# Two gate rows formed as columns and spread over the partitions through a DRAM row, the last features of two tiles activated and turned together, and the order list made anew

## The chip, the cores and the metric

The kernel runs on one core of a Trainium2 chip. The metric is the device time of one execution in microseconds (us). Every ratio below compares runs in the fast state on the same chip.

## The reference, cut to what matters

One layer: a linear attention with a learned feature map, then a gated feed-forward network (FFN), both with a normalisation that a vector `c` modulates, and both with a gate on their way back into `x`.

```python
mod = (_silu(c) @ w_mod).reshape(c.shape[0], 6, 1, -1)   # c: 1x512, w_mod: 512x3072
sa, ca, ga, sb, cb, gb = (mod[:, 0], mod[:, 1], mod[:, 2], mod[:, 3], mod[:, 4], mod[:, 5])
h = _layernorm(x) * (1 + ca) + sa                        # x: 1x2048x512
x = x + ga * _A_ref(h, ...)                              # attention, 32 heads of 16, ends in @ wo
h = _layernorm(x) * (1 + cb) + sb
x = x + gb * (_silu(h @ w_gate) * (h @ w_up)) @ w_down   # 1376 features inside
```

The two gates `ga` and `gb` are rows of 512 numbers, the same for all 2048 tokens. The 1376 inner features of the FFN are ten blocks of 128 and a last block of 96, "the last features".

## The kernel before

Tokens go through in 16 tiles of 128. In the first phase GpSimd makes the key features `phik` of every tile, TensorE accumulates key by value (`kv_ps`) and forms the query projections (`q_front`). Then come the attention of a tile (`attend`, into the output bank `four_ps` of TensorE), its projection by `wo`, and the FFN. Every step is declared as an operation with the engine that takes it. A long list, `ORDER`, fixes for each engine the order of its operations, and a helper fills planned gaps of TensorE with multiplications of ones.

A gate is needed on all partitions. The kernel before gets it there in the matmul itself, whose stationary operand is one column repeated 128 times, so that every output partition holds the same row:

```python
gab = const.tile([P, 2, D], BF16, name="gab")

def gate(gi):
    col0 = (2 * D, 5 * D)[gi]
    t = bank("fold")
    def f():
        for k in range(KD):                                   # KD = 4, D = 512
            nc.tensor.matmul(t()[:], lhsT=silucT[:, k:k + 1].to_broadcast([P, P]),
                             rhs=wmod_sb[:, k, col0:col0 + D], start=(k == 0), stop=(k == KD - 1))
    pl.op("PE", ..., fn=f)
    pl.op("ACT", ..., fn=lambda: nc.scalar.copy(gab[:, gi, :], t()[:]))
...
for k in range(KD):                    # the first gate is multiplied into wo, on GpSimd or VectorE
    eng.tensor_tensor(wo_sb[:, k, :], wo_sb[:, k, :], gab[:, 0, :], op=ALU.mult)
```

The last features of a tile come out with tokens on partitions and have to be turned, that is transposed, which a DMA transfer does:

```python
def ffn_tail(unit, guT):               # unit: one tile or two
    for q in range(w):                 # each tile by itself
        ps_ = bank("gu", (P, 2 * lastf))
        ...                            # 8 matmuls of 96 columns: gate and up
        ... nc.scalar.activation(sg()[:], ps_()[:, 0:lastf], ACT.Silu)
        ... nc.vector.tensor_tensor(gul()[:, 0:lastf], ps_()[:, lastf:2 * lastf], sg()[:], op=ALU.mult)
        ... nc.sync.dma_start(gu()[:, q * P:(q + 1) * P], gul()[:], transpose=True)
```

All loads, stores and turns here but three small ones (64, 16 and 1 KB, on ScalarE's queue) go through SyncE's DMA queue, one issued behind the other. The weights `wo`, `wg`, `wu` and `wd` are loaded from about 36 us on.

The softmax here doesn't subtract the row's maximum and nothing guards it: scores larger than these inputs give would overflow.

## Time and profile before

| what | value |
|---|---|
| time, median of three runs | 208.27 us |
| span of the profiled run (it took 209.14 us, 0.9 us over the median) | 207.3 us |
| GpSimd: first to last key feature | 19.93 to 56.20, 36.27 us |
| first scaling of `wo` on GpSimd | 56.20 us |
| first FFN matmul (L948) | 71.79 us |
| from there to the end | 207.3 - 71.79 = 135.5 us |

Since the start of an execution varies, points of time in two traces can differ by a microsecond for no reason; stretches are compared where it matters.

First, SyncE's timeline, with the start, the duration of the issue and the transfer, where the big weight loads are issued:

```profile
36.70 0.50 SPq L317 DMA_DIRECT2D wg_sb<-in_B_w_gate_dram  x1
37.24 0.51 SPq L317 DMA_DIRECT2D wu_sb<-in_B_w_up_dram  x1
37.79 7.96 SPq L317 DMA_DIRECT2D wd_sb<-in_B_w_down_dram  x2
```

Second, the DMA view, its total for the window from 42 to 54 us, in which these loads run:

```profile
DMA packets 2087, 3.20 MB, mean 266 GB/s; under 512 B 64, under 2 KB 1440, under 8 KB 2086
```

SyncE is held for 8 us by the issue of `wd`, where `wg` and `wu` took 0.5 us each; the data flow at 266 GB/s, which includes a slack end after all has landed.

### The profile page before, as it was taken

How to read it: one execution, taken by the hardware profiler on the slowest of the kernel's cores; microseconds unless marked ns; L12 is line 12 of the kernel's file. 1: busy time of each engine (PE TensorE's matmuls, PEld its weight loads, DVE VectorE, ACT ScalarE, POOL GpSimd, SP SyncE). 2: the span in 40 equal slices, each digit the busy share in tenths (PEclk: the TensorE clock that was granted, in tenths of full speed). 3: DMA queues.
4: the chain of work that ended last, by engine and by line, in shares of the span. 5: the costliest groups of instructions: out<-in, count | busy, mean ns of one | idle time of the engine just before them, and what ended most of it. 6: DMA issues, size and time to landing. Idle time of an engine off the chain costs nothing.

```text
span 207.3 us, 4949 instructions
## 1 busy us (share of the span) xinstructions
PE 202.4 (98%) x1876; PEld 140.0 (68%) x1876; DVE 143.1 (69%) x351; ACT 114.0 (55%) x244; POOL 131.0 (63%) x172
## 2 busy tenths in 40 slices
PE   7999999999999999999999999999999999999994
PEld 2764656454555698785887876879675787698752
DVE  6699899999676886999789687887467222322232
ACT  2689999998789974335452542422532564044300
POOL 1069999899991546689678793677749254061451
PEclk9999999999999999999999999999999999999999
DMA  5996993797000011231611233202321330020012
GB/s 176 335 389 119 321 191 87 275 406 254 4 0 0 3 25 36 51 81 26 91 32 28 58 83 81 57 0 60 79 62 28 79 85 3 13 66 27 0 34 68
DMA packets 34025, 19.76 MB, mean 95 GB/s; under 512 B 25073, under 2 KB 30674, under 8 KB 34002
## 3 DMA queue, kind: packets, MB, share of 16 engines
q1 hardware_dynamic: 33712, 19.38, 33.5%
q8 instruction: 14, 0.23, 0.5%
q10 hardware_dynamic: 290, 0.08, 0.2%
q14 instruction: 9, 0.07, 0.1%
HBM read 11.58 MB, written 2.10 MB: 66 GB/s over the span
## 4 chain that ended last, share of the span: by engine, by line
PE 92%; DMA 2%; ACT 1%; POOL 1%; DVE 1%; SPq 0%; issue 0%; DVEq 0%
PE one_ps L906 34%; PE one_ps L978 18%; PE one_ps L852 7%; PE one_ps L613 6%; PE one_ps L673 6%; PE one_ps L617 5%; PE four_ps L781 4%; PE one_ps L948 3%; PE kv_ps L1046 2%; DMA wqkv_sb<-in_A_wqkv_dram 2%; PE kv_ps L649 2%; PE one_ps L447 1%; PE one_ps L551 1%; PE one_ps L540 1%; ACT e L624 1%; POOL phik L642 1%
## 5 line engine op out<-in xcount | busy, mean ns | idle before, releaser
L978 PE MATMUL one_ps<-wd_sb,gu 128*128 128x512 bf16 (+2 forms) x176 | 41.0, 372 | 0.0
L906 PE MATMUL one_ps<-hT,wg_sb 128*128 128x256 bf16 (+1 forms) x400 | 41.0, 251 | 0.0
L906 PE MATMUL one_ps<-hT,wu_sb 128*128 128x256 bf16 (+1 forms) x400 | 40.9, 251 | 0.0
L913 ACT ACTIVATE sg<-one_ps 128x512 bf16<-128x512 f32 (+1 forms) x42 | 23.7, 576 | 27.6 <-PE one_ps L906 26.4
L906 PEld LDWEIGHTS <-wg_sb 128*128 128x128 bf16 x400 | 32.7, 98 | 4.8
L906 PEld LDWEIGHTS <-wu_sb 128*128 128x128 bf16 x400 | 32.9, 98 | 4.2
L916 DVE TENSOR_TENSOR gu<-one_ps,sg 128x512 bf16<-128x512 f32 (+1 forms) x26 | 16.6, 640 | 22.1 <-PE one_ps L906 12.8
L642 POOL TENSOR_TENSOR phik<-e,R 128x1024 bf16<-128x1024 bf16 x16 | 30.5, 1930 | 1.1 <-ACT eT L679 0.7
L922 POOL TENSOR_TENSOR gu<-usb,sg 128x512 bf16<-128x512 bf16 x16 | 18.5, 1155 | 16.8 <-ACT sg L913 13.3
L978 PEld LDWEIGHTS <-gu 128*128 128x128 bf16 (+1 forms) x187 | 17.7, 98 | 15.0
L384 DVE BATCH_NORM_STATS2 st<-x_c 128x6 f32<-128x512 bf16 x32 | 21.3, 682 | 1.4 <-DMA x_c<-in_A_x_dram 1.1
L994 POOL TENSOR_TENSOR ot<-x_c,fg 128x512 bf16<-128x512 bf16 (+1 forms) x14 | 15.7, 1118 | 8.8 <-DVE fg L990 8.8
L839 POOL TENSOR_TENSOR o<-o 128x512 bf16<-128x512 bf16 x14 | 16.1, 1154 | 7.6 <-DVE o L819 7.1
L819 DVE TENSOR_TENSOR o<-four_ps,A 128x512 bf16<-128x512 f32 x32 | 20.5, 683 | 0.0
L634 DVE TENSOR_REDUCE S<-e 128x64 f32<-128x1024 bf16 x16 | 19.0, 1194 | 0.6 <-ACT e L624 0.4
L624 ACT ACTIVATE e<-one_ps 128x512 bf16<-128x512 f32 x32 | 17.7, 631 | 1.6 <-POOL phik L642 1.0
L990 DVE TENSOR_TENSOR fg<-one_ps,gab 128x512 bf16<-128x512 f32 (+1 forms) x16 | 10.7, 672 | 11.5 <-PE one_ps L978 10.8
L679 ACT ACTIVATE eT<-one_ps 128x512 bf16<-128x512 f32 x32 | 17.5, 628 | 1.4 <-PE one_ps L673 1.3
L920 ACT CAST usb<-one_ps 128x512 bf16<-128x512 f32 x16 | 9.3, 586 | 16.3 <-PE one_ps L906 14.4
L852 PE MATMUL one_ps<-wo_sb,oT 128*128 128x512 bf16 x64 | 16.1, 379 | 0.0
L617 PE MATMUL one_ps<-wqkv_sb,hT 128*128 128x512 bf16 x64 | 15.9, 379 | 0.1
L673 PE MATMUL one_ps<-hT,Wq 128*128 128x512 bf16 x64 | 15.6, 379 | 0.1
(117 smaller groups left out, 311.2 us busy)
## 6 DMA issues: line engine op xcount, KB each, us to landing
wmod_sb<-in_w_mod_dram SPq DMA_DIRECT2D x2, 1024.0 KB, 7.0
out_dram<-ot SPq DMA_DIRECT2D x15, 128.0 KB, 2.0
wg_sb<-in_B_w_gate_dram SPq DMA_DIRECT2D x1, 1376.0 KB, 8.3
wu_sb<-in_B_w_up_dram SPq DMA_DIRECT2D x1, 1376.0 KB, 11.3
wd_sb<-in_B_w_down_dram SPq DMA_DIRECT2D x1, 1280.0 KB, 14.4
x_c<-in_A_x_dram SPq DMA_DIRECT2D x4, 256.0 KB, 4.7
wmod_sb<-in_w_mod_dram SPq DMA_DIRECT2D x4, 256.0 KB, 5.7
wqkv_sb<-in_A_wqkv_dram SPq DMA_DIRECT2D x2, 512.0 KB, 7.1
```

Of the source, the lines that this page charges most:

```text
L384: pl.op("DVE", r=reads, w=[st6], us=0.6, fn=lambda: nc.vector.bn_stats(st6()[:], src))
L617: nc.tensor.matmul(v()[:], lhsT=hT[c_i][k][:, cols], rhs=wqkv_sb[:, k, 2 * D:3 * D], start=(k == 0), stop=(k == KD - 1))
L624: nc.scalar.activation(e()[:, :, sg].rearrange("p g h f -> p g (h f)"), pk()[:].rearrange("p (g n) -> p g n", g=G), ACT.Exp, scale=(1.0, - ...
L634: pl.op("DVE", r=[e], w=[Ss], us=1.14, fn=lambda: nc.vector.tensor_reduce(Ss()[:], e()[:].rearrange("p g s h f -> p (g s h) f"), axis=AX.X ...
L642: pl.op("POOL", r=[e, R], w=[bphik[i]], us=1.92, fn=lambda: nc.gpsimd.tensor_tensor(bphik[i]()[:].rearrange("p g s h f -> p (g s h) f"), e ...
L673: nc.tensor.matmul(pq()[:], lhsT=Wq2[:, k, j * P:(j + 1) * P], rhs=hT[c_i][k][:], start=(k == 0), stop=(k == KD - 1))
L819: nc.vector.tensor_tensor(o2()[:, sg].rearrange("p j (h d) -> p j h d", d=DH), ndv()[:, :, sg, 0:P].rearrange("p j (h d) -> p j h d", d=DH ...
L852: nc.tensor.matmul(a()[:], lhsT=oT()[:, j, :], rhs=wo_sb[:, j, :], start=(j == 0), stop=(j == KD - 1))
L906: nc.tensor.matmul(ps_()[0:fsz, q * n:(q + 1) * n], lhsT=wt[:, k, m * P:m * P + fsz], rhs=h2[k], start=(k == 0), stop=(k == KD - 1))
L913: pl.op("ACT", r=[g, btab], w=[sg], us=0.08 + 0.41 * L / CW, fn=lambda: nc.scalar.activation(sg()[0:fsz, 0:L], g()[0:fsz, 0:L], ACT.Silu))
L922: pl.op("POOL", r=[usb, sg], w=[gu], us=0.17 + 0.98 * L / CW, fn=lambda: nc.gpsimd.tensor_tensor(gu()[0:fsz, 0:L], usb()[0:fsz, 0:L], sg() ...
L978: nc.tensor.matmul(fp()[:], lhsT=b()[0:fsz, c0:c0 + P], rhs=wd_[0:fsz, m, wcs], start=(m == 0), stop=(m == FM - 1))
```

## The change

The intent is to take matmul time from TensorE and small steps from the other engines. A gate becomes 16 one-column matmuls, which give it as four columns of 128 (`gcol`, 128x4). A store writes these as a row of 512 numbers into DRAM, and a load reads that row back onto all 128 partitions. In units of two tiles the last features share one activation, one multiplication and one turn. The order list was made anew.

```diff
+    grow = dram.tile([2, D], BF16, name="grow")              # a row in DRAM for each gate
     def gate(gi):
-        t = bank("fold")
+        t = bank("fold", [P, KD])
+        col = const.tile([P, KD], BF16, name=f"gcol{gi}")
             for k in range(KD):
-                nc.tensor.matmul(t()[:], lhsT=silucT[:, k:k + 1].to_broadcast([P, P]), rhs=wmod_sb[:, k, col0:col0 + D], ...)
+                for j in range(KD):
+                    nc.tensor.matmul(t()[:, j:j + 1], lhsT=wmod_sb[:, k, col0 + j * P:col0 + (j + 1) * P],
+                                     rhs=silucT[:, k:k + 1], ...)
-        pl.op("ACT", ..., fn=lambda: nc.scalar.copy(gab[:, gi, :], t()[:]))
+        pl.op([("ACT", ...), ("DVE", 0.12, lambda: nc.vector.tensor_copy(col[:], t()[:]))], ...)
+        nc.sync.dma_start(grow[gi:gi + 1, :].rearrange("a (j p) -> p (a j)", p=P), col[:])
+        nc.sync.dma_start(gab[:, gi, :], grow[gi:gi + 1, :].broadcast_to([P, D]))
     def ffn_tail(unit, guT):
-        for q in range(w):                                   # 16 activations, multiplications and turns
+        ps_ = bank("gu", (P, w * 2, lastf))                  # 10 of each
         ...
+        nc.scalar.activation(sg()[:, 0:w, :], ps_()[:, 0:2 * w:2, :], ACT.Silu)
+        nc.vector.tensor_tensor(gul()[:, 0:w, 0:lastf], ps_()[:, 1:2 * w:2, :], sg()[:, 0:w, :], op=ALU.mult)
+        nc.sync.dma_start(gu()[:, 0:w * P]..., gul()[:, 0:w, :]..., transpose=True)
     ... (buffer counts; the order list replaced whole)
```

In the store, partition p holds the elements p, 128 + p, 256 + p and 384 + p of the row. So no two neighbours in DRAM come from the same partition: the 1 KB goes out as 512 separate writes of two bytes.

## The prediction

> **What bounds the kernel now.** I read the page first: engine shares, the slices, the chain that ended last. Then the chain in order of time, the lines of the operations that the change touches, and GpSimd's and SyncE's timelines.
>
> ```profile
> span 207.3 us, 4949 instructions
> PE 202.4 (98%) x1876; PEld 140.0 (68%) x1876; DVE 143.1 (69%) x351; ACT 114.0 (55%) x244; POOL 131.0 (63%) x172
> ...
> PE 92%; DMA 2%; ACT 1%; POOL 1%; DVE 1%; SPq 0%; issue 0%; DVEq 0%
> ```
>
> TensorE is busy from end to end, and 92% of the chain is TensorE's own work. No other engine is above 69%. So a change pays if it takes matmul time away, or time in which TensorE fills a wait. The kernel does fill: its helper at L1046 multiplies ones into an unused bank wherever its plan sees a gap, so a busy TensorE can hide a wait. The chain in order of time shows the gates (L692) and the two fills that matter here:
>
> ```profile
> 33.09 0.78 PE one_ps L492 x32
> ...
> 53.10 0.86 PE one_ps L692 x4
> ...
> 56.21 0.52 PE kv_ps L649 x16
> 56.73 0.86 PE one_ps L692 x4
> ...
> 70.36 0.65 PE one_ps L1046 x3
> 71.01 0.23 PE one_ps L447 x4
> 71.23 0.50 PE four_ps L781 x8
> 71.73 0.22 PE one_ps L1046
> ```
>
> Each gate is four 512-column matmuls, 0.86 us, and both lie on the chain. L492 forms the other modulation values as columns already: 32 one-column matmuls in 0.78 us. After the first projections TensorE fills for 0.65 + 0.22 = 0.87 us; from 72 us to 203 us no fill remains, the stretch is matmuls back to back.
>
> The first phase has a second bound. GpSimd's timeline:
>
> ```profile
> 19.93 1.93 POOL L642 TENSOR_TENSOR phik<-e,R 128x1024 bf16<-128x1024 bf16 x1
> 21.84 2.28 POOL L434 TENSOR_SCALAR xn<-x_c,ln_mv,ln_nmr 128x512 bf16<-128x512 bf16 x3
> ...
> 46.77 9.48 POOL L642 TENSOR_TENSOR phik<-e,R 128x1024 bf16<-128x1024 bf16 x5 [0.30 <-PE kv_ps L649]
> 56.20 4.49 POOL L736 TENSOR_TENSOR wo_sb<-wo_sb,gab 128x512 bf16<-128x512 bf16 x4
> ```
>
> From 19.93 to 56.20 it makes the 16 key features with hardly a gap, and the last one frees the last key-value accumulation (56.21 on the chain). TensorE and GpSimd end this phase together. The third bound, the end, is the last matmul near 204 us, two VectorE steps and a store.
>
> The operations of the last features (L952, L954, L957):
>
> ```profile
> L952 ACT ACTIVATE sgl<-one_ps 128x96 bf16<-128x96 f32 x16 | 4.0, 249 | 15.6 <-PE one_ps L948 15.5
> L954 DVE TENSOR_TENSOR gul<-one_ps,sgl 128x96 bf16<-128x96 f32 x16 | 3.9, 243 | 7.1 <-ACT sgl L952 7.0
> L957 SPq DMA_TRANSPOSE gu<-gul x16: 1093/1182/1235, 79.8 to 185.2; - x16
> ```
>
> They are on three engines with room, and none of the three shows on the chain; TensorE never waits there for a turned tile.
>
> **What the Trainium skill says.** (1) "TensorE: Matmul & The Clock Gate", section "Wait — 56ns, not 53.3ns?": a warm matmul starts N / 2.4 GHz plus about 2.5 ns after the one before, and never less than about 25 ns. The trace agrees: 0.86 / 4 = 215 ns at 512 columns, 0.78 / 32 = 24 ns at one. (2) "DMA: Bandwidth & Descriptors", section "Anatomy of one DMA — SWDGE (gpsimd) path": a transfer has a fixed cost of about 2 us, mostly the receipt of the write. Here the route is SyncE's, but the 128 KB stores land after 2.0 us and the turns after 2.3. (3) Same page, "Rules for kernel authors": a strided last dimension is lowered to one descriptor per element, and a transfer that reads what another wrote must wait for its completion. The gate's column store is such a scatter (512 elements of two bytes), and its spreading load waits for it; no line of this trace shows a store of that shape. (4) "ScalarE: Activation LUTs", "Rules for kernel authors": about 0.3 us for an ACTIVATE plus 0.83 ns an element. The trace has Silu at 249 ns for 96 columns and 597 for 512, so 0.84 ns an element and only 0.17 us fixed; I use the trace.
>
> **The change part by part.** The diff also replaces the whole order list, so I decoded both lists into operations (entry divided by four is the operation, remainder the engine chosen), after inserting four new transfers and dropping four of eight steps in each of six two-tile units. It fits: 981 operations become 961, each named once.
>
> Gates on TensorE: out 2 x 4 x 215 ns = 1.72 us, in 2 x 16 x 24.4 ns = 0.78 us. Saved 0.94 us, all of it TensorE time.
>
> Gates elsewhere: two 586 ns ScalarE copies go; two VectorE copies of 128x4 come (about 0.15 us each, an estimate from the 173 ns of a 128x4 ScalarE operation here). Four transfers come on SyncE's queue. The gates move from just before and after the last key-value accumulation to the sixth and seventh key tiles, near 31 to 34 us by counting the work ahead of them. The column stores sit in the queue behind the load of wo and between the large weight loads, which SyncE issues from 36.1 us; the data of those runs until about 52 us (38.5 + 14.4 for wd). The spread rows are queued behind them, so I expect them at 48 to 54 us. The scaling of wo needs the first after the last key feature, near 55; its result is needed at the first projection (65.96 before, scaling done at 60.7). So about 5 us of slack: hidden.
>
> Last features: same 128 matmuls of 96 columns on TensorE, saved 0. ScalarE: 16 x 0.249 = 4.0 us becomes 4 x 0.249 + 6 x (0.249 + 96 x 0.84 ns) = 3.0. VectorE: 3.9 becomes 4 x 0.243 + 6 x (0.243 + 96 x 1.05 ns) = 3.0 (1.05 ns from 681 ns at 512 columns). SyncE: 16 turns of 1.18 us become 10; the 512-column turns of xn take 1.21, so a pair should cost as one. All of this lies beside TensorE: 0 us of the span.
>
> The new order: two fewer query projections stand before the last key-value accumulation, 12 instead of 10 after it. GpSimd's share before it falls by two normalisations (2.28 / 3 = 0.76 each) and gains one modulation of the same shape and operation (counted as 0.76 too), so its stretch can shrink by 0.76 us, and by its 1.15 us of idle at most more (36.27 less 16 x 1.91 and 6 x 0.76). I take 1.0 us. TensorE has 0.94 us less up to the first FFN matmuls, plus up to 0.87 us of fill that the two projections can replace: 1.8 us if TensorE alone counted. GpSimd's bound says 1.0, as the work after the accumulation grows by 2 x 0.86 less one gate = 0.87, which only takes the place of the fill. I put the gain of this phase at 1.3 us. Ten of the residual additions move from GpSimd to VectorE (437 against 1153 ns), in a stretch where neither sets the pace: 0. The end has the same form: half tile, add, store: 0.
>
> Sum: 208.3 - 1.3 = 207.0 us.
>
> **The rivals.** First: GpSimd binds alone and the gates save nothing visible, being replaced by more fill before the accumulation. For it: GpSimd's gapless row. Against: it loses work too. Time 207.5 to 208.3. Second: everything adds, 0.94 + 0.87 and the 1.5 us of fill that TensorE shows around 20 to 23 us. For it: the order was searched anew. Time about 205.0. Third: the DRAM way is late. The two-byte scatter or a queue blocked behind wd (its second piece took 7.27 us to issue) brings the rows past 60 us, and the first projection waits. For it: this store is unmeasured; against: the slack. Time 209 to 212. Fourth: a pair's turn waits for both tiles and sits at the head of SyncE's queue (one oT turn took 8.77 us for two here), and the last third of a down projection waits. Against: the tail is placed ahead of most of its unit's other matmuls. Plus 0.5 to 2 us.
>
> **Range and chances.** Median 207.0; 8 in 10 between 205.2 and 208.9: the low end is nearly the second rival, the high end a small new wait of the third or fourth that eats the saving. 2% is 4.2 us: faster would need under 204.1, below the whole of the second rival: 4%. Slower needs over 212.4, a late gate row of the worst kind: 4%. Within: 92%.
>
> **What would show it.** Right: 32 one-column gate matmuls at about 24 ns, 0.39 us a gate, near 31 to 34 us; the first wo scaling starting within a us of the last key feature's end, not on a DMA; the last key-value accumulation ending 0.5 to 1.5 us earlier; the fill before the first FFN matmuls gone or smaller; no fill from there to the last matmul; ten turns of about 1.2 us. Wrong: GpSimd idle before the wo scaling with the gate row as releaser, TensorE idle in the FFN stretch, a turn of a pair near 2.4 us, or a later first key tile than 13.4 us.

## The result, and the profile after

| | before | after |
|---|---|---|
| median of the fast runs of this comparison | 208.27 us | 235.11 us (233.99 to 235.65, 4 runs) |
| ratio, 95% interval | 1 | 1.1277 [1.121, 1.1345] |
| span of the profiled run | 207.3 us | 232.2 us |
| first FFN matmul | 71.79 us | 96.63 us |
| from there to the end | 135.5 us | 135.6 us |

A ratio here is the mean time of one kernel's fast runs over that of the other's of the same rounds, so it is not quite the ratio of the medians quoted. Executions over 1.5% slower than the fastest of the same kernel are left out of the means. The changed kernel is 12.8% slower, where 207.0 us was predicted. The last row says where to look: the whole loss lies before the first FFN matmul.

SyncE's timeline after, for the same loads:

```profile
40.75 0.37 SPq L703 DMA_DIRECT2D grow<-gcol  x1
41.17 0.50 SPq L316 DMA_DIRECT2D wg_sb<-in_B_w_gate_dram  x1
41.72 0.50 SPq L703 DMA_DIRECT2D grow<-gcol  x1
42.26 0.51 SPq L316 DMA_DIRECT2D wu_sb<-in_B_w_up_dram  x1
42.81 10.61 SPq L316 DMA_DIRECT2D wd_sb<-in_B_w_down_dram  x1
55.94 17.08 SPq L705 DMA_DIRECT2D gab<-grow  x1
```

The first store of 1 KB is issued at 40.75, after SyncE has waited 4.8 us for VectorE's copy into the column; the load that waits for its landing is issued at 55.94, and even its issue takes 17 us. My reading is that the queue ahead of it doesn't drain. The chain that ended last, in order of time (start, duration, what), goes exactly through these two:

```profile
40.75 15.13 DMA grow<-gcol
...
55.94 26.15 DMA gab<-grow
...
85.37 1.12 PE four_ps L792 x8
```

The list of waits (engine, what it was to write, what it waited for, us in total, times, longest) shows who stood still meanwhile:

```profile
POOL wo_sb L747 <- DMA gab<-grow: 25.2, 1, 25.2
DVE wo_sb L747 <- DMA gab<-grow: 22.3, 1, 22.3
...
PE four_ps L792 <- DVE o L830: 21.0, 1, 21.0
```

GpSimd and VectorE both wait for the gate row, to scale `wo`. VectorE has one of the four scalings, and in its order this stands ahead of the attention of the first tile. While it waits, the attention bank isn't emptied, and TensorE stands idle for 20.97 us. When it resumes, its clock is low: the eight matmuls of L792 took 1.12 us here and 0.50 before, and the page's row of granted clock (tenths of full speed, 40 slices of the span) shows it:

```profile
PEclk9999999999995558999999999999999999999999
```

The Trainium skill has this in "TensorE: Matmul & The Clock Gate", section "What's actually happening": an idle TensorE drops to half its clock and needs some microseconds of work to get it back. The trace agrees, with 1.12 us against 0.50.

And the DMA view's total for the window from 42 to 54 us, to be held against the line of before:

```profile
DMA packets 161, 0.43 MB, mean 36 GB/s; under 512 B 5, under 2 KB 5, under 8 KB 161
```

In the same 12 us in which 3.20 MB had moved before, 0.43 MB moved, although the weights were waiting in the queue. So while the slow stores were under way, everything else crawled too: `wg` landed after 31.6 us (8.3 before) and `wd` after 39.0 (14.4 before).

### The profile page after: what moved, and what is told of

The parts are those of the page before. It is cut to its first block, busy times and chain, and to the rows that moved or that the text cites. A ratio compares the mean times of both kernels' runs of the same rounds, so it can differ in the third digit from the quotient of the medians.

```text
span 232.2 us, 4944 instructions
## 1 busy us (share of the span) xinstructions
PE 203.3 (88%) x1876; PEld 141.6 (61%) x1900; DVE 143.6 (62%) x352; ACT 118.4 (51%) x242; POOL 119.9 (52%) x159
## 4 chain that ended last, share of the span: by engine, by line
PE 72%; DMA 20%; DVE 3%; ACT 2%; issue 1%; SPq 1%; DVEq 0%; ACTq 0%
PE one_ps L917 30%; PE one_ps L988 16%; DMA gab<-grow 11%; DMA grow<-gcol 7%; PE one_ps L863 6%; PE four_ps L792 3%; PE one_ps L612 3%; PE kv_ps L1055 3%; DMA wqkv_sb<-in_A_wqkv_dram 2%; PE one_ps L958 2%; PE one_ps L616 2%; PE one_ps L672 2%; DVE S L633 1%; PE one_ps L446 1%; ACT e L623 1%
## 5 line engine op out<-in xcount | busy, mean ns | idle before, releaser
L988 PE MATMUL one_ps<-wd_sb,gu 128*128 128x512 bf16 (+3 forms) x166 | 39.5, 372 | 0.5
L917 PE MATMUL one_ps<-hT,wu_sb 128*128 128x256 bf16 (+1 forms) x400 | 39.5, 251 | 0.0
L933 POOL TENSOR_TENSOR gu<-usb,sg 128x512 bf16<-128x512 bf16 x16 | 18.4, 1154 | 34.3 <-ACT sg L924 23.6
L792 PE MATMUL four_ps<-KVZ,eT 128*128 128x144 bf16 x128 | 11.1, 232 | 21.0 <-DVE o L830 21.0
L792 PEld LDWEIGHTS <-eT 128*128 128x128 bf16 x128 | 9.3, 100 | 23.3 <-issue 21.5
L678 ACT ACTIVATE eT<-one_ps 128x512 bf16<-128x512 f32 x32 | 16.8, 650 | 2.3 <-PE one_ps L672 2.3
L747 POOL TENSOR_TENSOR wo_sb<-wo_sb,gab 128x512 bf16<-128x512 bf16 x3 | 3.6, 1226 | 25.2 <-DMA gab<-grow 25.2
L672 PE MATMUL one_ps<-hT,Wq 128*128 128x512 bf16 x62 | 16.1, 394 | 0.3 <-issue 0.2
## 6 DMA issues: line engine op xcount, KB each, us to landing
wg_sb<-in_B_w_gate_dram SPq DMA_DIRECT2D x1, 1376.0 KB, 31.6
```

The costliest lines, as they stand in the source:

```text
L672: nc.tensor.matmul(pq()[:], lhsT=Wq2[:, k, j * P:(j + 1) * P], rhs=hT[c_i][k][:], start=(k == 0), stop=(k == KD - 1))
L792: nc.tensor.matmul(nd()[:, j, sg * NDW:(sg + 1) * NDW], lhsT=eTs[c_i, sg, j][:, ts_], rhs=KVZ[:, sg * KD + j, :], start=True, stop=True)
L917: nc.tensor.matmul(ps_()[0:fsz, q * n:(q + 1) * n], lhsT=wt[:, k, m * P:m * P + fsz], rhs=h2[k], start=(k == 0), stop=(k == KD - 1))
L933: pl.op("POOL", r=[usb, sg], w=[gu], us=0.17 + 0.98 * L / CW, fn=lambda: nc.gpsimd.tensor_tensor(gu()[0:fsz, 0:L], usb()[0:fsz, 0:L], sg() ...
L988: nc.tensor.matmul(fp()[:], lhsT=b()[0:fsz, c0:c0 + P], rhs=wd_[0:fsz, m, wcs], start=(m == 0), stop=(m == FM - 1))
```

## The experiments

Fifteen kernels ran, each beside runs of the kernel before on the same chip. First come those on the large loss, then those on the store's time, then those on the rest.

### Is it the gates' way through DRAM, or the order?

**The changed kernel with the old gates.** Its order list and joined last features stay; the gates are formed by the old matmuls, and the two transfers of each become empty steps.

```diff
-                for j in range(KD):
-                    nc.tensor.matmul(t()[:, j:j + 1], lhsT=wmod_sb[:, k, col0 + j * P:...], rhs=silucT[:, k:k + 1], ...)
+                nc.tensor.matmul(t()[:], lhsT=silucT[:, k:k + 1].to_broadcast([P, P]), rhs=wmod_sb[:, k, col0:col0 + D], ...)
-        pl.op("XBAR", r=[b], w=[br], ...store...)
-        pl.op("XBAR", r=[br], w=[bgab[gi]], ...load...)
+        pl.op("NONE", r=[b], w=[br], us=0.0, fn=lambda: None)
+        pl.op("NONE", r=[br], w=[bgab[gi]], us=0.0, fn=lambda: None)
```

> The changed kernel with its own order list and its joined last features, but each gate formed as before, by four 512-column matmuls into a bank of all partitions and one copy (VectorE) into the gate tile; the two transfers are empty steps. Theory (the gates' way through DRAM is the whole loss): within 1% of the kernel before, 206.5 to 209.5 us, TensorE never idle for over 1 us after 14 us. Rival (the new order or the joined last features cost a good part): 213 us or more.

Measured: 210.33 us, ratio 1.0096 [1.0077, 1.0116], correct. Without the way through DRAM nearly the whole loss is gone, 235.1 to 210.3. The ratio is within the 1% that the theory allowed, the time 0.8 us past its 209.5, since the new order is no gain either: it costs some 2 us, and I come back to it.

**The kernel before with the new gates alone.** The opposite: old order, old last features, only the column gates with store and load, at the old place late in the first phase, when no weights are under way any more.

```diff
-            nc.tensor.matmul(t()[:], lhsT=silucT[:, k:k + 1].to_broadcast([P, P]), rhs=wmod_sb[:, k, col0:col0 + D], ...)
-        ... nc.scalar.copy(gab[:, gi, :], t()[:])
+            ... 16 one-column matmuls, copy to gcol, store to grow, load to gab, as in the change
```

> The kernel before with only the gates changed: columns, store of two-byte elements to DRAM, spreading load, right behind each other, all in the old order, where no weight load is under way any more (those end near 52 us, the gates come at 53 and 57). Theory (the store itself takes about 15 us until it has landed, whatever else runs): store to landing 14 to 17 us each, the first wo scaling waits until about 72 to 76 us, 217 to 230 us in all. Rival (the store is slow only because weight loads stand around it in the queue): landing in 2 to 4 us, 207 to 211 us in all.

Measured: 239.22 us, ratio 1.1492 [1.1457, 1.1527], correct. SyncE's timeline:

```profile
53.35 0.38 SPq L698 DMA_DIRECT2D grow<-gcol  x1
67.55 0.34 SPq L700 DMA_DIRECT2D gab<-grow  x1
67.99 0.39 SPq L698 DMA_DIRECT2D grow<-gcol  x1
89.24 0.33 SPq L700 DMA_DIRECT2D gab<-grow  x1
```

This is the cleanest measurement of the store. With no weight load beside it, it takes 67.55 - 53.35 = 14.2 us for 1 KB. So it isn't slow because it stands behind weights; it is slow by itself. The second took 21.2 us; why it took longer than the first I don't know. The kernel's total missed the expected 217 to 230 us: by the list of waits GpSimd stood another 17.3 us for the second row, to scale `wd`, and TensorE 14.1 us for a normalisation on GpSimd.

**All scalings of `wo` on GpSimd.** In the changed kernel, the one on VectorE moves to GpSimd (one entry of the order list).

```diff
-  1100, 1096, 1309, 1364,
+  1100, 1096, 1308, 1364,
```

> The changed kernel with all four scalings of wo on GpSimd, none on VectorE, where one stood ahead of the first tile's attention and held VectorE until the gate row came. If that place makes TensorE wait earlier than the gate row needs: TensorE does the next attention and some query projections during the wait, 230 to 234 us in place of 235. If the wait for the row is all that counts: within 0.7 us of the changed kernel.

Measured: 235.42 us as the median of its three fast runs (232.27 to 235.51), ratio 1.1231 [1.1162, 1.1299], correct; its profile fell in the slow state, so I use it only to see who waits:

```profile
PE one_ps L858 <- POOL wo_sb L742: 20.5, 2, 18.9
```

The time stays, within the noise of these runs. TensorE now gets past the attention and waits at the first projection for the scaled `wo`. So VectorE's place in the order isn't the cause, only the place where the late row was felt first.

### What is slow in the store?

Four kernels change only where the store's writes fall. Their gates come out wrong, since the load takes the row in the wrong order or reads a row of `w_mod` in its place: the times count, not the results.

**Runs of eight bytes.** The four numbers of a partition go side by side into the same 1 KB (the wrong order for the gate).

```diff
-            grow[gi:gi + 1, :].rearrange("a (j p) -> p (a j)", p=P), col[:]))
+            grow[gi:gi + 1, :].rearrange("a (p j) -> p (a j)", p=P), col[:]))
```

> The changed kernel, but each partition's four elements go to four neighbouring places of the row: 128 runs of 8 bytes in place of 512 runs of 2, same bytes, same 1 KB of DRAM (the gate values come in the wrong order: wrong result on purpose). Theory (a fixed cost of about 30 ns for each short run written, one after the other: 15.4 us / 512): a store holds the memory about 3.8 us, the first gate row lands near 56 to 60 us, 207 to 212 us in all. Rival (the time is a latency of the whole store, or goes with the bytes): as slow as the changed kernel, 230 us or more.

Measured: 210.64 us, ratio 1.0123 [1.0073, 1.0173].

**Two-byte writes, each in a line of 512 bytes of its own.** As many writes as in the change, but over 256 KB.

```diff
-    grow = dram.tile([2, D], BF16, name="grow")
+    grow = dram.tile([2, KD, P, 256], BF16, name="grow")
-            grow[gi:gi + 1, :].rearrange("a (j p) -> p (a j)", p=P), col[:]))
+            grow[gi, :, :, 0:1].rearrange("j p w -> p j w"), col[:].unsqueeze(2)))
-            gab[:, gi, :], grow[gi:gi + 1, :].broadcast_to([P, D])))
+            gab[:, gi, :], w_mod[0:1, 0:D].broadcast_to([P, D])))
```

> The changed kernel, but each two-byte element goes to a 512-byte line of its own (512 lines in place of one 1 KB row), and the spreading load waits for the store as before but reads a row of w_mod (wrong result on purpose). Theory A (each short run costs about 30 ns wherever it goes): as the changed kernel, 230 to 238 us, store 14 to 17 us. Theory B (the runs are slow because they fall into the same few lines of memory, one after the other): the store lands in 2 to 5 us and the kernel takes 206 to 212 us.

Measured: 210.75 us, ratio 1.0112 [1.0076, 1.0149].

**The same at 64 bytes** (one look only, so its state is unknown) **and at 8 bytes.**

```diff
-    grow = dram.tile([2, KD, P, 256], BF16, name="grow")
+    grow = dram.tile([2, KD, P, 32], BF16, name="grow")      # 64 bytes apart
+    grow = dram.tile([2, KD, P, 4], BF16, name="grow")       # 8 bytes apart, in a kernel of its own
```

> As the run with a 512-byte line for each element, but with 64 bytes for each: 512 two-byte runs over 32 KB (wrong result on purpose). If 64 bytes are enough to keep the runs apart: store lands in 2 to 3 us, 209.5 to 212 us. If the runs queue up by larger pieces of memory: eight runs share each 512 bytes, the store takes 3 us or clearly more, and up to 14 us if they queue by 4 KB or more.

> The changed kernel with its 512 two-byte writes eight bytes apart: 4 KB, so 64 lines of 64 bytes with 8 writes in each; the spread row is read from w_mod, so the result is wrong on purpose. Measured so far: 512 writes in 1 KB (32 in a 64-byte line) 14.2 us alone, 128 writes in 1 KB (8 in a line) 3.6 us, 512 writes at 64 bytes or more (1 in a line) 2.1 us. Theory 1, writes into one 64-byte line go one after another and lines go side by side: the store lands after what 8 in a line cost, about 3.6 us, and the kernel takes 210 to 211.5 us. Theory 2, writes into one small region go one after another whatever the line, at 28 ns each: 512 x 28 ns = 14 us again (longer beside the weights, 33 us before), and the kernel stays at 225 to 236 us. Theory 3, a larger line, of 512 bytes: 64 writes in a line would be twice the 32 of the store of before per unit of 512 bytes in 8 units rather than 2: 4 times shorter than theory 2 by units, so about 14 x 64/256 = 3.6 us too; this run does not separate it from theory 1, but the one at 64 bytes' spacing (8 in a 512-byte unit, 2.1 us) speaks only weakly against it.

Measured: 210.27 us at 64 bytes; 212.2 us, ratio 1.0177 [1.0156, 1.0198], at 8 bytes. The times of these four kernels hardly differ, so the store itself has to be read. The view of its line gives the time from issue to landing of the two stores (the least, the middle, the greatest); the least is the first store. In this order: the changed kernel, runs of eight bytes, 8 bytes apart, 512 bytes apart.

```profile
DMA to landing us min/median/max: 15.1/24.0/33.0
```

```profile
DMA to landing us min/median/max: 3.6/7.2/10.7
```

```profile
DMA to landing us min/median/max: 3.9/7.5/11.1
```

```profile
DMA to landing us min/median/max: 2.1/4.6/7.1
```

| writes | spacing | writes in 64 bytes | first store lands after |
|---|---|---|---|
| 512 of 2 bytes | 2 bytes | 32 | 15.1 us beside weights, 14.2 alone |
| 128 of 8 bytes | 8 bytes | 8 | 3.6 us |
| 512 of 2 bytes | 8 bytes | 8 | 3.9 us |
| 512 of 2 bytes | 64 bytes | 1 | 2.1 us |
| 512 of 2 bytes | 512 bytes | at most 1 | 2.1 us |

The number of writes doesn't set the time: 512 take anything from 2.1 to 15.1 us. Nor does their size: rows two and three differ in both size and number and agree. What goes with the time is how densely the writes lie: 15.1 / 32 = 0.47 us, 3.6 / 8 = 0.45 and 3.9 / 8 = 0.49 us for each write in a stretch of 64 bytes (all beside weights), and below that a floor of about 2.1 us. The second theory of the last expectation, one queue for a small region at 28 ns a write, is refuted, since it wanted 14 us there; the first named 3.6 us and 3.9 came, though the kernel's 212.2 us is a little past the 211.5 that it allowed. My reading is that short writes close together wait for each other, while stretches apart go side by side. How large such a stretch is these runs don't tell, since all spacings were even; the counts per 512 bytes would fit just as well. Nor do they tell where the writes wait, in the memory or on the way to it.

The second half of the damage also goes. The DMA total from 42 to 54 us with 512 bytes between the writes, where the changed kernel had 36 GB/s:

```profile
DMA packets 2775, 4.04 MB, mean 337 GB/s; under 512 B 565, under 2 KB 1750, under 8 KB 2774
```

The short writes of a store went out in this window (565 packets under 512 bytes) and the weights flowed. At 8 bytes apart the same window had 215 GB/s, in between. So it isn't short writes as such that starve the other transfers, but short writes that lie close together. Whether weights in another queue would have flowed beside the dense store was not tried.

**The change with the store mended.** This one is correct. If each matmul takes every fourth column of the weight, partition p gets the elements 4p to 4p + 3 of the gate, and the store is 128 runs of eight bytes in the right order.

```diff
-                    nc.tensor.matmul(t()[:, j:j + 1], lhsT=wmod_sb[:, k, col0 + j * P:col0 + (j + 1) * P], ...
+                    nc.tensor.matmul(t()[:, j:j + 1], lhsT=wmod_sb[:, k, col0 + j:col0 + D:KD], ...
-            grow[gi:gi + 1, :].rearrange("a (j p) -> p (a j)", p=P), col[:]))
+            grow[gi:gi + 1, :].rearrange("a (p j) -> p (a j)", p=P), col[:]))
```

> The changed kernel whole (new order, joined last features, columns, DRAM row), mended in one place: column j takes every fourth weight column, so that each partition's four values are neighbours of the row and the store is 128 runs of 8 bytes; the result is right. If the short runs into the same lines are the cause of the 26 us: as the run with 8-byte runs, 209.5 to 211.5 us, so within 1.5% of before, still not faster; store about 3.6 us. If the stride of the weight columns slows TensorE's loads, a gate takes over 0.6 us instead of 0.4.

Measured: 211.54 us, ratio 1.0146 [1.0114, 1.0178]. By the ratios it recovers 23.6 of the 26.6 us. The store lands after 3.7 us. A gate's 16 matmuls now take 0.54 us (30.56 to 31.10) and not 0.40: the strided weight columns cost something, less than the 0.6 us feared. GpSimd's timeline still has a wait for the row, which now stands behind the weights in the queue:

```profile
61.17 3.61 POOL L747 TENSOR_TENSOR wo_sb<-wo_sb,gab 128x512 bf16<-128x512 bf16 x3 [4.74 <-DMA gab<-grow]
```

This wait of 4.74 us costs little: TensorE idles 0.51 us for VectorE ahead of the second attention, and reaches the FFN at 73.82.

### What the rest of the change is worth

**Joined last features alone**, in the kernel before and its order.

```diff
-        for q in range(w):                      # per tile: activation, multiplication, turn
+        ps_ = bank("gu", (P, w * 2, lastf))     # per unit, as in the change; the order list with the doubled steps dropped
```

> The kernel before with the joined last features alone, each joined step standing in the old order where the later of its two tiles stood. Prediction's step (all beside TensorE, 0 us): within 0.3 us of before, 10 turns of about 1.2 us each. Rival (joining makes the down projections wait, this is the residue of 2 us that the new order shows): 209.5 us or more, with TensorE idle after 72 us.

Measured: 208.52 us, ratio 0.999 [0.9969, 1.0011], correct. It is worth nothing that shows, as predicted.

**Mended gates alone**, in the kernel before, formed early (about 33.5 us) so that the row has time.

```diff
     def gate(gi):                               # as in the mended change above
+        ... lhsT=wmod_sb[:, k, col0 + j:col0 + D:KD], rhs=silucT[:, k:k + 1], ...
+        ... grow[gi:gi + 1, :].rearrange("a (p j) -> p (a j)", p=P), col[:]
 # order list: both gates behind the other modulation values, stores behind the load of wo, spreading loads behind wd
```

> The old order and the old last features, with the mended gates alone (8-byte runs), moved up behind the modulation columns at about 34 us, so that their rows are there in time. Theory (TensorE's 0.94 us comes out, as predicted, when no wait stands in its place): 207.2 to 207.9 us against 208.4 of before. Rival (GpSimd's row of key features sets the end of the first phase, the saved matmul time becomes waiting or fill): 208.1 to 209 us.

Measured: 210.73 us, ratio 1.01 [1.008, 1.0121], correct. The rows landed in time (by 56.8 us), and still 2 us were lost, which neither expectation had. GpSimd's timeline (start, duration, work, and in brackets the idle time ahead and what ended it):

```profile
39.62 7.72 POOL L636 TENSOR_TENSOR phik<-e,R 128x1024 bf16<-128x1024 bf16 x4 [1.52 <-DVE R L634]
```

I read it so: the gates' matmuls, and a fill of 0.44 us behind them, now stand ahead of a key tile on TensorE, that tile is late (35.04, before 33.73), and GpSimd waits 1.52 us. Its stretch from the first to the last feature is 57.27 - 19.73 = 37.54 us in place of 36.27.

**The gates at a quarter.** The kernel before with one of the four matmuls of each gate, 6 x 216 ns = 1.3 us of TensorE less. Its output is wrong, which doesn't matter for the time.

```diff
-            for k in range(KD):
+            for k in range(1):
```

> The kernel before, untouched but for the gates: each is formed from one quarter of its sum, one 512-column matmul in place of four (wrong result on purpose), at its old place in the order. That takes 6 x 0.215 = 1.3 us of matmul time away there and adds nothing. If the gates' matmul time was on TensorE's path, as the prediction had it: about 207.1 us. If it stood where TensorE would wait anyway (for GpSimd's last key features and for the key-value matrix behind them): 208.2 to 208.7 us.

Measured: 208.98 us, ratio 1.0016 [0.9987, 1.0045]; 207.1 us would have been 0.994, and the median is 0.3 us past the 208.2 to 208.7 of the second theory. From the first key feature to the first FFN matmul the trace has 71.09 - 19.25 = 51.84 us, before 71.79 - 19.93 = 51.86. TensorE's timeline shows where a part of the saved time went, just ahead of the first attention:

```profile
58.47 0.66 PE L781 MATMUL four_ps<-KVZ,eT 128*128 128x144 bf16 x8 [0.38 <-DVE KVZ L751]
```

TensorE is now early and waits for VectorE, which makes `KVZ` out of the accumulation. Matmul time of a gate, taken away at this place, is worth nothing that shows.

**One feature more on GpSimd.** The kernel before, making the key features of tile 10 twice: 1.93 us more for GpSimd.

```diff
-        ... nc.gpsimd.tensor_tensor(bphik[i]..., op=ALU.mult))
+        ... [nc.gpsimd.tensor_tensor(bphik[i]..., op=ALU.mult) for _ in range(2 if i == 10 else 1)])
```

> The kernel before, but GpSimd forms the key features of tile 10 twice (same result, 1.93 us more on GpSimd, nothing more on any other engine). If GpSimd sets the end of the first phase: 210.0 to 210.8 us, 1.6 to 2.1 us more than before, and its last key feature ends near 58 us. If GpSimd has slack there: 208.3 to 209.2 us.

Measured: 210.25 us, ratio 1.0069 [1.0035, 1.0103], correct: 0.0069 x 208.4 = 1.4 us of the 1.93. GpSimd's timeline has the last feature end at 57.55:

```profile
57.55 4.49 POOL L736 TENSOR_TENSOR wo_sb<-wo_sb,gab 128x512 bf16<-128x512 bf16 x4
```

Its stretch grew by 1.66 us (57.55 - 19.62 = 37.93), and from its end to the first FFN matmul it took 15.59 us, exactly as before. So GpSimd, though busy only 63% of the whole span, sets the end of the first phase.

**A modulation moved back.** The changed kernel with the old gates shows GpSimd idle ahead of a modulation (L585) that the new order gave it:

```profile
32.77 0.77 POOL L585 TENSOR_SCALAR hT<-raw,modA 128x512 bf16<-128x512 bf16 x1 [2.78 <-PE one_ps L612]
```

I moved this step behind the next key feature, one entry of the list.

> The run with the old gates in the new order, but on GpSimd the one modulation of chunk 2 stands behind the key features of tile 6 and not ahead of them. In that run GpSimd idles 2.8 us ahead of this modulation while tile 6's sums are ready some 2 us earlier. If this place in the new order eats GpSimd's saving: the last key feature ends 1 to 2 us earlier and the kernel takes 208.4 to 209.5 us in place of 210.3. If the residue of the new order has another cause: 210 us or more.

Measured: 210.64 us, ratio 1.0099 [1.0071, 1.0127], no gain over the 1.0096 without it. The gap broke into three of 0.71, 0.90 and 0.94 us, in which GpSimd waited for TensorE and VectorE. My theory, that the modulation's place alone made the gap, fell: the features were not ready either. (The stretch of features was 36.88 us here, 37.27 without the move, and the time didn't follow.)

**Less for GpSimd.** Two attempts at a kernel that beats both: the kernel before with joined last features, and one first normalisation (0.76 us on GpSimd) given to VectorE, or to ScalarE (each one entry of the list).

```diff
-  661, 654, 658, 666, 608,
+  661, 654, 658, 664, 608,      # VectorE
+  661, 654, 658, 665, 608,      # ScalarE, in a kernel of its own
```

> A candidate to beat both: the kernel before with joined last features, and one of GpSimd's first normalisations of the last chunk (0.76 us of its gapless stretch) given to VectorE, which takes about 0.35 us for it. If GpSimd alone sets the end of the first phase, 0.76 us come off it and the kernel gains up to 0.55 us by the ratio measured when I added 1.93 us and lost 1.4: 208.0 us against 208.5, ratio 0.997. If VectorE's chain (sums and reciprocals of the key features) feeds GpSimd without slack there, the 0.35 us delay a key feature and the gain is nothing: ratio 0.999 to 1.001.

> The same, with that normalisation on ScalarE (0.74 us there) in place of VectorE. If GpSimd alone sets the end of the first phase: ratio 0.997, 208.0 us. If ScalarE, which is nearly without gaps from 27 to 40 us, then feeds VectorE and GpSimd later, it gives the gain back: ratio 1.000 to 1.003.

Measured: 209.42 us, ratio 1.0053 [1.0035, 1.0071], and 208.78 us, ratio 1.0021 [1.0007, 1.0034], both correct. Both intervals lie just above 1, far below the 2% that counts as slower here; the first is outside its expectation. GpSimd's timeline with the step on VectorE:

```profile
34.24 1.93 POOL L635 TENSOR_TENSOR phik<-e,R 128x1024 bf16<-128x1024 bf16 x1 [1.38 <-DVE R L633]
```

GpSimd lost 0.76 us of work and gained 1.38 us of waiting for VectorE's reciprocals in one place. In both tries a step taken from GpSimd and given to an engine that feeds it was a small loss. No version that I tried beats the kernel before.

## Why the prediction was wrong, point by point

**The gates on TensorE: the durations right, their worth wrong.** A gate took 0.39 us by the prediction; in the trace, the 16 matmuls of the first start at 31.80 and the next work at 32.20, 0.40 us (the second gate came at 36.04, a little after the 31 to 34 us expected). The copies on VectorE took 148 ns, estimated at 150. But the step "Saved 0.94 us, all of it TensorE time" was counted as time of the span. The quarter gates took more than that away, in the old order, and gained nothing. As I read it, the chain of TensorE's work looked unbroken because it ran at the pace of GpSimd's features and VectorE's `KVZ`, with just as much to do as there was time. The prediction's first rival, "GpSimd binds alone and the gates save nothing visible", was right about this.

**The gate rows: the step that failed.** It said "So about 5 us of slack: hidden", with the rows on the partitions at 48 to 54 us. In fact the first came at 82.08 us. The prediction had read from the Trainium skill ("DMA: Bandwidth & Descriptors", "Rules for kernel authors") that such a store is lowered to one descriptor per element, had said that no line of the trace shows such a store, and then gave it no duration of its own: the only stores that it quotes land after about 2 us. It measured 14.2 us alone and 15.1 beside the weights, whose transfers were held up with it. The slack itself was about right: with runs of eight bytes and in the mended change the row came 4.46 and 4.74 us after the last feature, and in their traces TensorE idled 0.23 and 0.51 us for it. So what failed is the time of the landing, not the 5 us. The third rival, "The DRAM way is late", has the right mechanism and is the term that was mis-sized: it was given 209 to 212 us, a few microseconds past the slack, and 235 came. An unmeasured shape with 512 elements had deserved a wide tail, not 4% for slower.

**The last features: right.** 10 turns, median 1.17 us against the expected 1.2; ScalarE 2.9 us and VectorE 3.1 us, each expected at 3.0; and 0 of the span (ratio 0.999 alone). The fourth rival, a pair's turn that delays the down projections, didn't show: landing took 2.3 us in the middle, and from the first FFN matmul on both kernels take 135.5 to 135.6 us. (Of the residual additions eight moved to VectorE by the traces, GpSimd's 14 becoming 6, where the prediction counted ten.)

**The new order: wrong in sign.** Expected were 1.0 us less of GpSimd's stretch from the first to the last feature and a gain of 1.3 us in all. With the old gates in the new order the stretch is 56.65 - 19.38 = 37.27 us against 36.27, 1.0 us longer, and the kernel 2 us slower. In other traces of this order it is 36.6 to 37.4 us, so the size varies and the sign doesn't. The prediction counted the work given to GpSimd and took from it, and not whether the other engines feed it in time; the 2.78 us of idle are more than the 0.76 us of work that it lost. The rest of the loss can be read from the two traces: from the last feature to the first FFN matmul 73.51 - 56.65 = 16.86 us against 71.79 - 56.20 = 15.59, the steadier part of the loss (16.9 us also in the runs with 64 and 512 bytes between the writes). In that part, two more query projections (2 x 0.86 us) stand in place of a gate and a fill (0.86 + 0.65), and from the transposes on TensorE (L446) to the FFN it takes 1.33 us (72.18 to 73.51) where it took 0.78, waiting for ScalarE's modulation; some 0.5 us of the 1.27 these don't explain. These are readings, not tests; the one test, the modulation moved back, gained nothing, so what in the new order starves GpSimd stays open in part.

**The sum.** Expected -1.3 us; measured on the traces +24.9 us. Of this TensorE's idle stretch is 20.97 us, the new order about 2, and the rest mostly the slow restart at half clock (the first 16 matmuls took 1.12 + 0.85 us against 0.50 + 0.45, and six projections after them 2.04 us, where six at 0.86 / 4 take 1.29).

**What would show it wrong.** The first of the signs named, "GpSimd idle before the wo scaling with the gate row as releaser", is the line that the list of waits shows, with 25.2 us.

## What to carry to other kernels

Before a value goes to DRAM as a scatter of single elements, look at how densely its writes lie, and choose which elements a partition gets, so that its run is as long as can be: with the order of the matmul columns changed, the same store fell from 15.1 to 3.7 us, for 0.14 us more of each gate on TensorE. A transfer of a shape that the trace doesn't show has no duration yet; measure it alone before counting on slack, and count with it slowing its neighbours. And time taken off the engine that is busiest overall bought nothing in a phase where it followed another, so add work to the suspected engine first and see whether the end moves.

## What the Trainium skill lacked or had wrong

- "DMA: Bandwidth & Descriptors": its section "Rules for kernel authors" says that transfers under 64 KB are mostly overhead and that a strided last dimension becomes one descriptor per element, but no rule says that short writes close together in DRAM wait for each other. Here 1 KB took 14.2 us as 512 writes of two bytes side by side, 3.6 us as 128 writes of eight bytes, and 2.1 us as 512 writes 64 or 512 bytes apart.
- The same page, "Why small descriptors are slow (HBM only)": it names costs of the small descriptor itself. Those can't be the main cause here, since 512 equally small writes took 15.1, 3.9 or 2.1 us by their spacing alone. The page's specifications mention a read-modify-write below 512 bytes, which could be a reason for writes of one stretch to wait for each other; no run here shows it, and it isn't said there that it serialises neighbours.
- The same page, no section on a core's own stores ("Back-pressure in remote DMA" speaks of transfers between cores): while such a store is under way, the other transfers of the core starve. Over 12 us 36 GB/s moved, against 337 GB/s with the same number of short writes 512 bytes apart.
- The same page, "Anatomy of one DMA — SWDGE (gpsimd) path": the fixed cost of about 2 us fits the spread stores (2.1 us) and the turns (2.3 us) on SyncE's queue too, and is seven times too small for the dense store.
- "ScalarE: Activation LUTs", "Rules for kernel authors": about 0.3 us fixed for an activation; the two shapes of Silu here (249 ns at 96 columns, 597 ns at 512) give 0.17 us.
